# Conv taps and gated product kept in SBUF instead of PSUM, with other load buffers and another job order, in an attention and gated-projection kernel on one core

## The chip, the core and the metric

The kernel runs on one core of a Trainium2 chip. The metric is device time in microseconds (us), lower is better. The core's engines have queues of their own: TensorE (PE for the matmuls, PEld for the weight loads ahead of them), VectorE (DVE), ScalarE (ACT), GpSimd (POOL) and SyncE (SP, which issues the DMAs). PSUM is the memory that TensorE writes; SBUF is the large memory that all engines work in.

## What is computed

Rotary attention over 8 batches of 8 heads (sequence 576, head size 64), then a gated projection of the joined heads (width 512): a causal convolution of five taps per channel makes a gate, which multiplies a projected value, and a second projection gives the output.

```python
q_rot, k_rot = (rotate(q), rotate(k))
scores = scale * np.matmul(q_rot, k_rot.transpose(0, 1, 3, 2))
scores = scores - np.max(scores, axis=-1, keepdims=True)
attn = np.exp(scores)
attn = attn / (np.sum(attn, axis=-1, keepdims=True) + 1e-09)
x = np.matmul(attn, v)                      # heads joined: (8, 576, 512)
xp = np.concatenate([np.zeros((B, K - 1, D)), x], axis=1)
for k in range(K):                          # K = 5
    gate_pre += conv_w[k][None, None, :] * xp[:, k:k + S, :]
gate = 1.0 / (1.0 + np.exp(-gate_pre))
val = x @ w_val
return gate * val @ w_out
```

## The kernel before

**Tiling.** The 64 heads are 32 pairs `p`; a pair fills the 128 partitions. Four pairs make a batch `b`. Everything is transposed: channels on partitions, positions along the row. Matmul operands are split in a coarse part and a remainder (`hi`, `lo`), and three products of them are added, so most steps exist twice.

**One pair, in jobs.** `load` brings k and q, and `load_v` the values. `rope_mul` (two), `rope_add`, `qk_hi` and `qk_lo` make the rotated, split operands. `s_mm` computes the scores of two heads for 128 queries (12 matmuls, into two PSUM units), with `s_mix` for what is left over; `s_max` takes the row maximum on DVE and `s_exp` the exponential on ACT. `t_mm` turns the exponentials on TensorE, `t_copy` copies them to SBUF, `pv_mm` and `pv_left` multiply them with v, and `x_norm` writes the scaled result x. The reciprocal sums travel by `r_copy`, `r_write`, `r_read`. `x_hi` and `x_lo` split x. Five `tap` jobs and `gate` (a tanh) make the pair's gate.

**One batch.** `f_mm` of stage 0 multiplies with `w_val` (8 jobs of 6 matmuls into one unit). `y_mul` forms (gate + 1) times that unit, `y_hi` and `y_lo` split the product. Stage 1 multiplies with `w_out`; `o_out` scales and `o_dma` stores.

**PSUM units.** PSUM is cut in four units (`u`, two banks each). A score job takes two, and `t_mm`, `pv_mm` with the rest of its pair, `f_mm` and, before the change, the first `tap` take one. A unit is free again when the last reader of what it holds is done. The taps add into `ps_c` in such a unit until `gate` has read it; `y_mul` writes back into the unit of its `f_mm`, and `y_hi` and `y_lo` read it there.

**What sets the order.** `ORDER` is a table of about 3,100 job numbers. The jobs are issued in this order; within an engine they run in it. A letter behind a number picks the engine where several can do the job (V, A, G for DVE, ACT, GpSimd), and the digits behind a colon are the buffers or units that the job takes. `FILLS` puts idle transposes on TensorE at some steps. `Plan.run` has one more rule: a GpSimd job whose kind stands in `PAIRED` waits for the last DVE job of those kinds ahead of it in the table. Nothing makes a later DVE job wait for GpSimd.

**Lines.** L364 and L374 score matmuls, L384 turns, L480 and L490 products with v, L602 projections, L389 `s_max`, L398 `s_exp`, L467/L469 `t_copy` (ACT/DVE), L567/L569/L570 taps (DVE later ones, first one on DVE, on ACT), L582 gate, L615 `y_mul`, L626/L627 `y_hi` (DVE/ACT), L631 `y_lo`, L301 `rope_mul`, L305 `rope_add`, L326/L327 `qk_hi`, L333 and L336 `qk_lo` of q and k, L545/L546 `x_hi`, L552 `x_lo`.

Of the kernel before, what the change touches and what calls it, by code (L numbers as in the profile page):

```python
# [34 lines left out]
40 45:0 4 115 43:0 57:3 105A 147 116 23 44:0 48:2 5 58:1 119A 51:1 46:2 141G 59:1 49:3 47:2 54:3 142V 50 60:0 52:0 143G 63:2 55:1 53 148V 144A 66:1  # L35
64:2 56:3 145G 61:3 65 76:3 149V 67<61 216 77A:0 72:2 41 150V 62 74:3 106 73A 151V 78:0 152 146 75A:0 117 157:2 223 82V:0 79A 68:0 160:3 158:1 217G 69
154:0 161:2 159:0 166:1 155:3 70 162:2 218G 83:2 80 71 167:0 156 163:3 107 81A 169:0 168:1 219V 85 6 170:1 225G 90:1 87:0 377:100 220A 88:0 164:2 92
171:3 221V 165 184:0 224V 86A 292 84A 178:3 110A 229 118 175:2 185A:1 108 226V 89:0 179<108 172:0 176:3 227A 120G 93 180:0 177 109 222 91 194A:1 181
173:1 294V 174 192:2 186:3 293V 195 190:0 187A:1 228 94 295V 191A 299 239:3 95 182 193A 121G 236:0 196A 240:2 378A 305 183 241:0 237:3 197 131 230:1
198V 379 199:1 188:3 238:2 296V 200:1 233:2 380 189A 231:0 251:0 297G 234:1 232 248:3 381 235 488 262:1 111V 254:2 249:2 263A:0 112G 252:3 250:1 242:1  # L40
# [186 lines left out]
def attn_gated_ffn(ctx: ExitStack, tc: tile.TileContext, q2, k2, v2, tab, w_val, conv_w, w_out, out, collect=None):  # L227
# [326 lines left out]
    def tap(p, k, a, b, eng=V):  # L554
# [4 lines left out]
        if k == 0:  # L559
            st[f"c{a}"] = unit("ps_c")  # L560
# [385 lines left out]
```

## Time and profile before

| | |
|---|---|
| time, median of 3 runs (lowest to highest) | 675.24 us (674.88 to 679.53) |
| the profiled execution's own time | 675.39 us |
| span of its instructions | 673.6 us |
| PE / PEld busy | 648.9 / 534.9 us (96% / 79%) |
| DVE busy | 559.3 us (83%), 858 instructions |
| ACT busy | 474.8 us (70%), 1016 instructions |
| POOL busy | 299.9 us (45%), 239 instructions |
| mean granted TensorE clock | 0.982 of full speed |

A share is busy time over the span. Ends of matmuls are modelled, so 96% for PE doesn't say that it ran at its best rate; weight loads (PEld) run ahead of the matmuls that use them, and a wait shows at them first. A row of waits reads: engine, output tile and line that waited, `<-` what ended the wait, total us, times, longest.

### The profile page before, as it was taken

The page shows a single profiled execution, that of the slowest core. Times are in us where ns is not written, and L with a number is a line of the kernel's source. Part 1 is how long each engine was busy: PE and PEld are TensorE (multiplying, and loading weights), DVE is VectorE, ACT ScalarE, POOL GpSimd, SP SyncE. Part 2 cuts the span into 40 slices and gives each one's busy share as a digit, 9 for nine tenths or more (in the row PEclk, how much of TensorE's full clock was granted, in tenths as well). Part 3 has the DMA queues.
Part 4 walks back from the last instruction along what each step waited for, and adds up shares of the span by engine and source line. Part 5 has one row for each costly group of instructions (what it writes and reads, how often), then busy time and mean ns, then how long its engine had stood idle before and what let it go on. Part 6 is the DMA issues. An engine that isn't in the chain of part 4 may idle for free.

```text
span 673.6 us, 21213 instructions
## 1 busy us (share of the span) xinstructions
PE 648.9 (96%) x8937; PEld 534.9 (79%) x8937; DVE 559.3 (83%) x858; ACT 474.8 (70%) x1016; POOL 299.9 (45%) x239
## 2 busy tenths in 40 slices
PE   8999799999999999999999999999999999999997
PEld 6876567878787887967887889788778789689796
DVE  5899988899988988978987978888888888887762
ACT  4888978788778677567867677786668655767421
POOL 1424566566546455462525458325656225240000
PEclk9799979999999999999999999999999999999999
DMA  7355532533433244322432433443135423301202
GB/s 223 108 179 150 151 115 72 159 108 114 139 111 91 55 127 146 107 81 89 145 99 77 127 127 109 130 143 101 46 107 145 129 76 107 107 21 37 70 25 71
DMA packets 42721, 72.85 MB, mean 108 GB/s; under 512 B 15449, under 2 KB 18050, under 8 KB 42626
## 3 DMA queue, kind: packets, MB, share of 16 engines
q1 hardware_dynamic: 42082, 70.91, 34.0%
q8 instruction: 70, 1.15, 0.7%
q10 hardware_dynamic: 544, 0.59, 0.3%
q14 instruction: 25, 0.20, 0.1%
HBM read 61.89 MB, written 9.59 MB: 106 GB/s over the span
## 4 chain that ended last, share of the span: by engine, by line
PE 75%; DVE 9%; ACT 9%; DMA 4%; issue 2%; SPq 1%; DVEq 0%; ACTq 0%
PE ps_f L602 26%; PE ps_a L480 18%; PE ps_s L364 15%; PE ps_t L384 9%; PE ps_s L374 4%; ACT p L398 3%; DVE nm L389 3%; ACT pt L467 3%; PE ps_a L490 2%; DVE ps_c L567 1%; DMA rb<-rd 1%; DMA wst<-in_w_val 1%; DMA tab<-in_tab 1%; PE ps_s L384 1%; DMA qin<-in_q 1%
## 5 line engine op out<-in xcount | busy, mean ns | idle before, releaser
L389 DVE TENSOR_REDUCE nm<-ps_s 128x1 f32<-128x576 f32 x288 | 206.5, 751 | 49.6 <-PE ps_s L364 37.0
L398 ACT ACTIVATE p<-ps_s,nm 128x576 f32<-128x576 f32 x256 | 188.1, 740 | 59.2 <-DVE nm L389 58.2
L364 PE MATMUL ps_s<-k,q 64*128 64x288 f32 x1536 | 160.2, 312 | 8.3 <-ACT pt L467 2.9
L364 PEld LDWEIGHTS ps_s<-k,q 64*128 64x128 f32 x1536 | 131.8, 191 | 31.6 <-ACT p L398 12.4
L480 PE MATMUL ps_a<-pt,v 128*64 128x320 f32 (+1 forms) x1024 | 139.6, 418 | 0.3 <-ACT p L398 0.2
L467 ACT COPY pt<-ps_t 128x1024 f32<-128x1024 f32 (+1 forms) x125 | 114.8, 941 | 19.3 <-PE ps_t L384 18.2
L301 POOL TENSOR_TENSOR kin<-kin,tab 128x576 f32<-128x576 f32 x52 | 73.4, 1421 | 91.6 <-DMA kin<-in_k 35.9
L602 PE MATMUL ps_f<-y,wout_hi 64*128 64x288 f32 (+2 forms) x1024 | 110.3, 301 | 1.4 <-ACT o L637 0.5
L480 PEld LDWEIGHTS ps_a<-pt,v 128*64 128x64 f32 x1024 | 69.5, 139 | 50.2 <-issue 9.1
L567 DVE SCALAR_TENSOR_TENSOR ps_c<-x,cw,ps_c 128x576 f32<-128x576 f32 (+2 forms) x132 | 105.0, 801 | 4.4 <-ACT ps_c L570 1.3
L384 PE MATMUL ps_t<-ident,p 64*128 64x64 f32 x2172 | 94.7, 225 | 3.2 <-ACT p L398 1.5
L384 PEld LDWEIGHTS ps_t<-ident,p 64*128 64x128 f32 x2172 | 85.7, 139 | 13.2 <-ACT p L398 7.8
L301 POOL TENSOR_TENSOR qin<-qin,tab 128x640 f32<-128x640 f32 x40 | 62.1, 1562 | 64.2 <-DMA qin<-in_q 34.3
L602 PEld LDWEIGHTS ps_f<-y,wout_hi 64*128 64x128 f32 x1024 | 84.4, 185 | 6.2 <-issue 1.2
L602 PE MATMUL ps_f<-xh,wval_hi 64*128 64x288 f32 (+2 forms) x512 | 86.3, 308 | 1.7 <-ACT p L398 0.8
L602 PE MATMUL ps_f<-xl,wval_hi 64*128 64x288 f32 (+2 forms) x512 | 82.0, 292 | 0.1
L602 PE MATMUL ps_f<-xh,wval_lo 64*128 64x288 f32 (+2 forms) x512 | 82.0, 291 | 0.0
L602 PE MATMUL ps_f<-y,wout_lo 64*128 64x288 f32 (+2 forms) x512 | 79.7, 291 | 0.0
L602 PEld LDWEIGHTS ps_f<-xh,wval_hi 64*128 64x128 f32 x512 | 54.8, 185 | 4.9 <-ACT p L398 1.0
L602 PEld LDWEIGHTS ps_f<-xl,wval_hi 64*128 64x128 f32 x512 | 54.8, 185 | 0.3 <-DVE xl L552 0.3
L602 PEld LDWEIGHTS ps_f<-xh,wval_lo 64*128 64x128 f32 x512 | 54.7, 184 | 0.0
L552 POOL TENSOR_TENSOR xl<-x,xh 128x576 fp32r<-128x576 f32 x25 | 35.6, 1424 | 41.7 <-ACT xh L546 32.9
(107 smaller groups left out, 882.7 us busy)
## 6 DMA issues: line engine op xcount, KB each, us to landing
kin<-in_k SPq DMA_DIRECT2D x31, 576.0 KB
qin<-in_q SPq DMA_DIRECT2D x31, 512.0 KB
v<-in_v SPq DMA_DIRECT2D x32, 320.0 KB
out_t<-o SPq DMA_DIRECT2D x28, 288.0 KB
rb<-rd SPq DMA_DIRECT2D x31, 144.0 KB
rb<-rd SPq DMA_DIRECT2D x31, 128.0 KB
wst<-in_w_val SPq DMA_DIRECT2D x4, 512.0 KB
o<-in_w_out SPq DMA_DIRECT2D x4, 512.0 KB
```

The costliest lines, as they stand in the source:

```text
L301: return eng.tensor_tensor(out=t[:, i, a:b], in0=t[:, 0 if p < RAW else i, a:b], in1=table[:, i, a:b], op=ALU.mult)
L364: T.matmul(out=tiles[h][:, half, 0:288], lhsT=st["q"][HEAD[h], x, c * 128:c * 128 + 128], rhs=st["k"][HEAD[h], y, k0 + half * 288:k0 + hal ...
L374: inst = T.matmul(out=st["s8"][:, half], lhsT=st["q"][HEAD[h], x, 512:640], rhs=st["k"][HEAD[h], y, D + half * 288:D + half * 288 + 288], ...
L384: T.transpose(out=bank[0:src.shape[1], x, k * D:(k + 1) * D], in_=src[rows], identity=ident[rows, rows])
L389: return V.tensor_reduce(out=st[f"nm{i}"], in_=st[f"s{i}"], axis=AX.XY, op=ALU.max, negate=True)
L398: return A.activation(out=to.rearrange("p (b x) -> p b x", b=2), in_=st[f"s{i}"], func=AF.Exp, bias=st[f"nm{i}"], scale=1.0, accum_out=sum ...
L467: return A.copy(out=dst, in_=src)
L480: T.matmul(out=st[f"a{g}"][HEAD[h], 0:n], lhsT=st["v"][:, j, h, :], rhs=st[f"pt{g}"][:, h * 4 + j], start=(j == 0), stop=False)
L490: T.matmul(out=st[f"a{x}"][HEAD[h], 0:n], lhsT=st["v"][rows, 4, h, :], rhs=st["ptr"][rows, h, 0:n], start=False, stop=True)
L552: return eng.tensor_tensor(out=st["xl"][:, a:b], in0=xs[p % NX][:, 4 + a:4 + b], in1=st["xh"][:, a:b].bitcast(F32), op=ALU.subtract)
L567: return V.scalar_tensor_tensor(out=acc, in0=x_sb, scalar=w, in1=acc, op0=ALU.mult, op1=ALU.add)
L602: inst = T.matmul(out=acc[:, x, 0:hi - lo], lhsT=wt[w][HEAD[h], kc, dc * 128:(dc + 1) * 128], rhs=mv[HEAD[h], lo:hi], start=(turn == 0 and ...
```

## The change

The taps add in SBUF, in the tile `g` that later holds the gate, and so need no unit. The first tap writes `g`, four more read x and `g` and write `g`, and `gate` works on it in place. `y_mul` reads `g` and the projection's unit and writes the product into `g`; `y_hi` and `y_lo` read that, and `y_lo` may run on GpSimd too (`GV` for `V`). `tap`, `y_hi` and `y_lo` join the kinds in `PAIRED`. There are three x buffers for four, two v buffers for three, two k load buffers for one. `FILLS` gets four more transposes at step 73. The order table is another one: the same 3,100 jobs, with 21 of 36 `y_lo` on GpSimd (none before), 106 `rope_mul` and `rope_add` there (142 before; the others are on DVE), 21 `x_lo` (25), 23 `qk_lo` (21); 27 of the first taps on ACT (22).

```diff
-NX = 4
+NX = 3
+NV = 2
+NIN = {"k": 2, "q": 1}
...
-7 24 8 11 17 0:0 35 10 12V 153 13V 113 14:0 18V 9 25V 15 19V 26V 20:1 30V 104 36V 27:2 37V 31V 140 1 32:3 28 21 29 2 38:2 3 22 33 16 114A 34 42:1 39
+7 24 8 11 17 0:0 35 10 12V 113 13V 14:0 25V 18V 15 26V 1 30V 27:1 104 19V 140 31V 28 20:2 9 2 3 36V 32:3 16 37V 21 38:0 22 29 114A 45:2 23 115 33 39
...
-FILLS = {12: (20, 0)}
+FILLS = {11: (20, 0), 73: (4, 0)}
...
-    PAIRED = ("rope_mul", "rope_add", "qk_hi", "qk_lo", "x_hi", "x_lo", "weight_step")
+    PAIRED = ("rope_mul", "rope_add", "qk_hi", "qk_lo", "x_hi", "x_lo", "tap", "y_hi", "y_lo", "weight_step")
...
-    ins = {n: const.tile([128, 2, wide[n]], F32, name=f"{n}in") for n in "kq"}
+    ins = {n: [const.tile([128, 2, wide[n]], F32, name=f"{n}in{i}") for i in range(NIN[n])] for n in "kq"}
...
-    vs = [const.tile([128, 5, 2, D], F32, name=f"v{i}") for i in range(3)]
+    vs = [const.tile([128, 5, 2, D], F32, name=f"v{i}") for i in range(NV)]
...
-        if k == 0:
-            st[f"c{a}"] = unit("ps_c")
-        if b - a == S:
-            acc = st[f"c{a}"][:, :, 0:288]
-            x_sb = x_sb.rearrange("p (x n) -> p x n", x=2)
-        else:
-            acc = st[f"c{a}"][:, 0, 0:b - a]
-        if k:
-            return V.scalar_tensor_tensor(out=acc, in0=x_sb, scalar=w, in1=acc, op0=ALU.mult, op1=ALU.add)
-        if eng is V:
-            return V.tensor_scalar(out=acc, in0=x_sb, scalar1=w, scalar2=None, op0=ALU.mult)
-        return A.activation(out=acc, in_=x_sb, func=AF.Copy, scale=w)
...
         if "g" not in st:
             st["g"] = ring("pg", [128, S], F32, "g")
         g = st["g"][:, a:b]
...
+        if k:
+            return eng.scalar_tensor_tensor(out=g, in0=x_sb, scalar=w, in1=g, op0=ALU.mult, op1=ALU.add)
+        if eng is A:
+            return A.activation(out=g, in_=x_sb, func=AF.Copy, scale=w)
+        return eng.tensor_scalar(out=g, in0=x_sb, scalar1=w, scalar2=None, op0=ALU.mult)
...
+        g = state[p]["g"][:, a:b]
+        return A.activation(out=g, in_=g, func=AF.Tanh, scale=0.5)
...
     def y_mul(b, two, dc, lo, hi):
-        acc, g = halves(two, ffn[b, 0, two[0]], dc, hi - lo, state[b * PPB + dc]["g"][:, lo:hi])
-        return V.scalar_tensor_tensor(out=acc, in0=g, scalar=1.0, in1=acc, op0=ALU.add, op1=ALU.mult)
+        acc, y = halves(two, ffn[b, 0, two[0]], dc, hi - lo, state[b * PPB + dc]["g"][:, lo:hi])
+        return V.scalar_tensor_tensor(out=y, in0=y, scalar=1.0, in1=acc, op0=ALU.add, op1=ALU.mult)
...
-        return V.tensor_tensor(out=rest, in0=acc, in1=y.bitcast(F32), op=ALU.subtract)
+    def y_lo(b, dc, lo, hi, eng):
+        return eng.tensor_tensor(out=y_part(b, 1)[:, dc, lo:hi], in0=state[b * PPB + dc]["g"][:, lo:hi],
+                                 in1=ffn[b][0][:, dc, lo:hi].bitcast(F32), op=ALU.subtract)
...
-                add("V" if k else "AV", tap, p, k, a, b, r=xr + " cw", w=f"u/c{p}.{g}")
-            add("A", gate, p, a, b, r=f"u/c{p}.{g}", w=f"pg/{p}{part}")
+                add("V" if k else "AV", tap, p, k, a, b, r=xr + " cw", w=f"pg/{p}{part}")
+            add("A", gate, p, a, b, w=f"pg/{p}{part}")
...
-                        add("V", y_lo, b, two, dc, x, y, r=f"{mine} y0/{to}", w=f"y1/{to}")
+                        add("GV", y_lo, b, dc, x, y, r=f"{mine} y0/{to}", w=f"y1/{to}")
```

Where the order moves: DVE first, in the middle of the program, while the scores of pairs 16 and 17 are computed. Before, the taps of pair 15 (x_88) and pair 14 (x_87) stand like this; `nm<-ps_s` is a row maximum, `x2` a count:

```order
L389 TENSOR_REDUCE nm<-ps_s 128x1 x2
L567 SCALAR_TENSOR_TENSOR ps_c<-x_88,cw,ps_c 128x2x288
L326 TENSOR_SCALAR k_71<-kin 128x576
L567 SCALAR_TENSOR_TENSOR ps_c<-x_88,cw,ps_c 128x2x288 x3
L638 TENSOR_SCALAR o<-ps_f 128x576
L507 RECIPROCAL pm<-sums_89 128x9
L333 SCALAR_TENSOR_TENSOR q_73<-qin,q_73 128x640
L567 SCALAR_TENSOR_TENSOR ps_c<-x_87,cw,ps_c 128x2x288 x4
L389 TENSOR_REDUCE nm<-ps_s 128x1 x2
```

In the changed kernel the same place, with the taps of pair 13 (x_86) written to `g` (the lines have moved: L391 is the maximum, L565 the taps, L303 `rope_mul`, L471 `t_copy`):

```order
L391 TENSOR_REDUCE nm<-ps_s 128x1 x2
L565 SCALAR_TENSOR_TENSOR g<-x_86,cw,g 128x576
L303 TENSOR_TENSOR kin_69<-kin_69,tab 128x576
L391 TENSOR_REDUCE nm<-ps_s 128x1 x2
L471 COPY pt_5323<-ps_t 128x8x64
L471 COPY pr<-ps_t 64x2x64
L629 TENSOR_SCALAR o<-ps_f 128x576
L471 COPY pt_5344<-ps_t 128x2x8x64
L391 TENSOR_REDUCE nm<-ps_s 128x1 x2
L565 SCALAR_TENSOR_TENSOR g<-x_86,cw,g 128x576
```

Taps that stood in a row of four between two pairs of maxima now stand one by one, with a maximum pair, copies and rope work between.

GpSimd second, in the same part of the program, around the remainder of x of pair 12 (`xl<-x_85`). Before, its jobs are rope work (L301, L305), remainders of k (L336) and of x (L552), and the sums (L498):

```order
L336 TENSOR_TENSOR k_72<-kin,k_72 128x576
L301 TENSOR_TENSOR kin<-kin,tab 128x576
L552 TENSOR_TENSOR xl<-x_85,xh 128x576
L301 TENSOR_TENSOR qin<-qin,tab 128x640
L305 TENSOR_TENSOR qin<-qin 128x640
```

In the changed kernel (L303, L307 rope, L338 k, L554 x, L621 `y_lo`):

```order
L303 TENSOR_TENSOR kin_69<-kin_69,tab 128x576
L307 TENSOR_TENSOR kin_69<-kin_69 128x576
L303 TENSOR_TENSOR kin_70<-kin_70,tab 128x576
L621 TENSOR_TENSOR y_4827<-g,y_4803 128x576 x2
L554 TENSOR_TENSOR xl<-x_85,xh 128x576
```

Remainders of the gated product (`y<-g,y`) have come to GpSimd, and the k rope work alternates between two load buffers (kin_69, kin_70).

## Rows read from the trace of the kernel before

**Rows 1.** Engines by stage: us, busy us (count) of each, PEclk, DMA share, GB/s
```profile
0.00:130.00 130.00, 118.38 (x1302) 94.55 (x1304) 112.09 (x195) 103.59 (x220) 61.38 (x54) 0.91 0.48 143
...
130.00:640.00 510.00, 501.98 (x7241) 414.22 (x7239) 430.85 (x627) 365.21 (x782) 238.54 (x185) 1.00 0.33 103
...
640.00:674.00 34.00, 28.54 (x402) 26.17 (x398) 16.36 (x38) 5.97 (x14) 0.00 (x0) 0.99 0.14 47
```
**Rows 2.** Waits of the weight loads: who <- for whom: us, times, longest
```profile
PEld ps_s L364 <- ACT p L398: 12.4, 31, 0.6
...
PEld ps_t L384 <- ACT p L398: 7.9, 18, 0.8
...
PEld ps_s L364 <- ACT pt L467: 6.1, 10, 1.0
...
PEld ps_t L384 <- ACT pt L467: 3.6, 5, 1.2
...
PEld ps_s L364 <- ACT g L582: 2.2, 2, 1.7
...
PEld ps_f L602 <- ACT p L398: 1.5, 2, 1.0
...
PEld ps_s L364 <- ACT pm L398: 1.4, 3, 0.5
...
PEld ps_t L384 <- ACT pr L467: 1.4, 2, 0.9
```
**Rows 3.** Groups by shape: the taps and the tanh, the first product, its remainder
```profile
L567 DVE SCALAR_TENSOR_TENSOR ps_c<-x,cw,ps_c 128x576 f32<-128x576 f32 x124 | 101.0, 819 | 4.1 <-ACT ps_c L570 1.3
...
L582 ACT ACTIVATE g<-ps_c 128x576 f32<-128x576 f32 x31 | 20.3, 654 | 22.6 <-DVE ps_c L567 19.8 <-PE ps_f L602 2.6
...
L326 DVE TENSOR_SCALAR k<-kin 128x576 fp32r<-128x576 f32 x11 | 5.2, 470 | 0.0
...
L631 DVE TENSOR_TENSOR y<-ps_f,y 128x576 fp32r<-128x576 f32 x28 | 21.0, 750 | 2.5 <-ACT y L627 2.2
```
**Rows 4.** Timeline around 305 us: start, duration, engine, line, op, tiles, xcount
```profile
302.42 1.42 DVE L389 TENSOR_REDUCE nm<-ps_s 128x1 f32<-128x576 f32 x2 [0.54 <-PE ps_s L364]
...
302.81 1.95 PE L480 MATMUL ps_a<-pt,v 128*64 128x256 f32 x16
...
304.68 0.66 PE L374 MATMUL ps_s<-k,q 64*128 64x288 f32 x6
...
305.19 0.95 PE L364 MATMUL ps_s<-k,q 64*128 64x288 f32 x12
...
308.00 1.20 PE L384 MATMUL ps_t<-ident,p 64*128 64x64 f32 x32
...
309.01 1.19 PE L364 MATMUL ps_s<-k,q 64*128 64x288 f32 x12
```
**Rows 5.** Groups by shape: line, engine, op, tiles, xcount | busy us, mean ns | idle before
```profile
L389 DVE TENSOR_REDUCE nm<-ps_s 128x1 f32<-128x576 f32 x288 | 206.5, 751 | 49.6 <-PE ps_s L364 37.0 <-PE ps_s L374 8.3 <-PE ps_t L384 1.3
...
L398 ACT ACTIVATE p<-ps_s,nm 128x576 f32<-128x576 f32 x256 | 188.1, 740 | 59.2 <-DVE nm L389 58.2
...
L467 ACT COPY pt<-ps_t 128x1024 f32<-128x1024 f32 x103 | 102.2, 1016 | 17.8 <-PE ps_t L384 16.9
```
**Rows 6.** Lines 567, 333 and 301: duration ns min/median/max, first and last start us
```profile
L567 DVE SCALAR_TENSOR_TENSOR ps_c<-x,cw,ps_c x132: 478/823/824, 72.5 to 647.4; 128x576 f32<-128x576 f32 x124, 128x256 f32<-128x256 f32 x4, 128x320 f32<-128x320 f32 x4
...
L333 DVE SCALAR_TENSOR_TENSOR q<-qin,q x31: 762/817/2030, 24.8 to 600.1; 128x640 fp32r<-128x640 f32 x31
...
L301 POOL TENSOR_TENSOR kin<-kin,tab x52: 1401/1422/1444, 15.1 to 590.3; 128x576 f32<-128x576 f32 x52
```
**Rows 7.** Timeline near 438 us: DVE and POOL rows that overlap
```profile
438.36 1.56 POOL L305 TENSOR_TENSOR qin<-qin 128x640 f32<-128x640 f32 x1 [0.76 <-DVE kin L301]
...
438.81 1.73 DVE L305 TENSOR_TENSOR kin<-kin 128x576 f32<-128x576 f32 x1
```
**Rows 8.** Waits of GpSimd's k rope work for the k loads: us, times, longest
```profile
POOL kin L301 <- DMA kin<-in_k: 35.9, 7, 9.5
```

More of the change, by code (lines that the diff above doesn't have):

```diff
@@ L37 @@
[L37 to L40, printed above, removed]
@@ L313, in rope_mm @@
             for i, m in enumerate((ident, swap.rearrange("p h i x -> p (h i x)"))):
-                T.matmul(out=bank[:, (x - a) // h, 0:h], lhsT=m, rhs=ins[n][:, i, x:x + h], start=(i == 0), stop=(i == 1))
+                T.matmul(out=bank[:, (x - a) // h, 0:h], lhsT=m, rhs=ins[n][p % NIN[n]][:, i, x:x + h], start=(i == 0), stop=(i == 1))
     def rotated(p, n, a, b):
-        return state[p][f"b{n}{a}"] if p < RAW else ins[n][:, 0, a:b]
+        return state[p][f"b{n}{a}"] if p < RAW else ins[n][p % NIN[n]][:, 0, a:b]
     def like(p, t):
@@ L621, in y_part, with y_hi @@
         return parts[x]
-    def y_hi(b, two, dc, lo, hi, eng):
-        acc, y = halves(two, ffn[b, 0, two[0]], dc, hi - lo, y_part(b, 0)[:, dc, lo:hi])
+    def y_hi(b, dc, lo, hi, eng):
+        hi_, y = y_part(b, 0)[:, dc, lo:hi], state[b * PPB + dc]["g"][:, lo:hi]
         if eng is V:
-            return V.tensor_copy(out=y, in_=acc)
-        return A.copy(out=y, in_=acc)
-    def y_lo(b, two, dc, lo, hi):
-        acc, y, rest = halves(two, ffn[b, 0, two[0]], dc, hi - lo, ffn[b][0][:, dc, lo:hi], y_part(b, 1)[:, dc, lo:hi])
-        return V.tensor_tensor(out=rest, in0=acc, in1=y.bitcast(F32), op=ALU.subtract)
+            return V.tensor_copy(out=hi_, in_=y)
+        return A.copy(out=hi_, in_=y)
+    def y_lo(b, dc, lo, hi, eng):
+        return eng.tensor_tensor(out=y_part(b, 1)[:, dc, lo:hi], in0=state[b * PPB + dc]["g"][:, lo:hi],
+                                 in1=ffn[b][0][:, dc, lo:hi].bitcast(F32), op=ALU.subtract)
     def o_out(b, two, oc, lo, hi, eng):
@@ L718, in attn_gated_ffn @@
             V.memset(x_sb[:, 0:4], 0.0)
-        V.memset(ins["q"][D:128, :, 512:S], 0.0)
-        V.memset(ins["q"][0:D, :, S:W], 0.0)
+        for t in ins["q"]:
+            V.memset(t[D:128, :, 512:S], 0.0)
+            V.memset(t[0:D, :, S:W], 0.0)
     add = plan.add
@@ L871, in attn_gated_ffn @@
                         gp = PPB * b + dc
-                        mine = f"{acc}#{dc}" if last else acc
-                        add("V", y_mul, b, two, dc, x, y, r=f"{acc} pg/{gp}" + (half if gp == NP - 1 else ""), w=mine)
-                        add("AV", y_hi, b, two, dc, x, y, r=mine, w=f"y0/{to}")
-                        add("V", y_lo, b, two, dc, x, y, r=f"{mine} y0/{to}", w=f"y1/{to}")
+                        mine = f"pg/{gp}" + (half if gp == NP - 1 else "")
+                        add("V", y_mul, b, two, dc, x, y, r=acc, w=mine)
+                        add("AV", y_hi, b, dc, x, y, r=mine, w=f"y0/{to}")
+                        add("GV", y_lo, b, dc, x, y, r=f"{mine} y0/{to}", w=f"y1/{to}")
                     else:
```

270 lines of the change are left out of this document (134 added, 136 removed).

## The prediction, made before the changed kernel ran

> **What bounds the kernel now.** I read the engines by stage first [rows 1]. In the middle stage, from 130 to 640 us, PE is busy 502 of 510 us at a granted clock of 1.00. DVE is busy 431 us and ACT 365. So TensorE sets the pace there, but it is not at its best rate, since the ends of matmuls are modelled. In the first 130 us it is different: PE and its loads do less, the granted clock is 0.91, and DVE is busy 112 us. The last stretch is 34 us of projections without POOL.
>
> What TensorE loses in the middle stands in the waits of the weight loads [rows 2]. A score matmul reads k and q alone. When it waits for an exponential (`ACT p`, 12.4 us) or a copy of turned blocks (`ACT pt`, 6.1 us), what it waits for is a PSUM unit that this reader had to leave. The same holds for turning matmuls that wait for `pt` or `pr`, for projections that wait for `p`, and for scores that wait for the gate (`ACT g`, 2.2 us). Turning matmuls that wait for `p` (7.9 us) wait for data or for a unit. The eight rows, which are of the whole span, make 12.4 + 7.9 + 6.1 + 3.6 + 2.2 + 1.5 + 1.4 + 1.4 = 36.5 us. That is the amount that an easier supply of units can give back.
>
> **What the change removes.** Per pair, the taps hold one of the four units: a first tap, four more of 0.82 us and a tanh of 0.65 [rows 3], at least 0.75 + 3.28 + 0.65 = 4.7 us, which is about 150 us over 32 pairs, of 4 x 674 unit-us. The stage-0 units are free after `y_mul` and no longer wait for `y_hi` and `y_lo`; the latter alone took 0.75 us, 28 times [rows 3].
>
> Does it help that units are held for 150 us less? Only if units come round later than before, and that I read from the two order tables. I gave each TensorE job its time from start to start of neighbours in the timeline [rows 4]. A score job of 12 takes 309.01 to 309.92 us by what follows it, so 0.9. A block of 16 turns takes half of 308.00 to 309.01, so 0.5. Half a product with v takes 0.93 for the narrow kind, half of 302.81 to 304.68; I take 1.2 for the wide one, 0.7 for its rest and 0.4 for a projection job, from their neighbours in the same stretch. Then I summed, for each unit that held scores, the TensorE work between its last matmul and the next job that gets the unit. The mean is 2.56 us over 275 such reuses before, and 2.98 over 288 after. For units that held turned blocks it is 1.67 us (151) and 2.02 (163).
>
> What a score unit needs is a maximum of 0.75 us and an exponential of 0.74 [rows 5]. The second unit of a job needs one maximum more, so the mean is 1.9 us. A turned block needs its copy, 1.02 us on ACT, so 1.1. The work lacking below 1.9 and 1.1 us adds up to 36 + 10 = 46 us before, which is close to the 36.5 us of waits. After it adds up to 24 + 6 = 30 us, a third less. **Term 1:** a third of 36.5 us, 12 us back. Bounds: nothing, where the wait only moves on to the next reader, and all 36.5.
>
> **DVE's own work.** A tap read x from SBUF and its sum from PSUM: 819 ns [rows 3]. With both in SBUF, the nearest row is line 333, the same kind of instruction on 640 columns, with a median of 817 ns [rows 6]; for 576 columns that makes some 0.75 us. So 124 taps save 8.7 us. A first tap on DVE goes from 0.82 us towards the 0.47 us of the k split, an SBUF to SBUF scaling [rows 3]. Against this, 36 rope instructions move to DVE at about 0.8 us (+28 us), and 21 `y_lo` leave it (-16 us). With the smaller moves (copies, outputs, splits) my sum for DVE is 8 us less than before. DVE is not the bound in the middle stage (431 of 510 us), so I count a third: **term 2**, 3 us back, between 0 and 8.
>
> **What it adds.** Contention between DVE and POOL. The taps of before have a minimum, median and maximum of 478, 823 and 824 ns [rows 6] although, by my count over the trace, 84 of the 124 full ones overlap a POOL job of over 1 us: with one operand in PSUM they are never held up. Line 333, with two inputs in SBUF, has a median of 817 and a maximum of 2030 ns [rows 6]. At 438.8 us a `rope_add` on DVE took 1.73 us while a POOL job of 1.56 us had begun 0.45 us before it [rows 7]; its usual time is 0.75. It ended just after that POOL job and its own 0.75 us. The changed taps, `y_hi` and `y_lo` become such instructions. `PAIRED` makes POOL start behind them; but the next one on DVE starts when its turn comes, and must sit out the rest of a POOL job of 1.42 us [rows 6].
>
> I counted how much POOL work is not covered, between one such DVE job and the next, by DVE work that can't collide (two maxima in a row cover 1.42 us [rows 4]). It is 22 us before and 54 after. In the trace of before, the DVE instructions above the usual time of their kind exceed it by some 8 us (some 18 instructions, of which the two named are examples), so about 0.4 of what is uncovered. 54 x 0.4 is 22 us, 14 more than now. A third of that on TensorE's path, as above, gives **term 3**, 4 to 5 us lost; bounds 0 and all 32 us more.
>
> The Trainium skill, in "SBUF — State Buffer", section "Who interferes with whom", says that a DVE instruction with two SBUF inputs and a GpSimd instruction that reads SBUF exclude each other, and that the second to issue waits for the whole of the first. The trace agrees in the row of 1.73 us. By that rule alone every uncovered microsecond is a wait, which is the rival below that ends slower.
>
> **Costed at nothing.** Two k load buffers: POOL's rope work waited 35.9 us for k loads [rows 8], but by the order the split k stands a mean of 17 us of TensorE work ahead of its scores; what hides the wait is POOL's idle time (239 of 510 us busy in the middle stage [rows 1]). If that cover went, the first score job of a pair would be late by one POOL job, 1.42 us. Fewer v and x buffers: v is still loaded a good 8 us of TensorE work ahead of its use, and the taps of a pair are done before x of the third next pair is written. Four fill transposes: under 1 us, in a stretch where TensorE waits for DVE. `gate` and the first taps on ACT change by some 0.03 us each. The first 130 us: DVE has the same work ahead of pair 4's end in both orders (102 and 101 us in my sum), so I give no gain there; nor in the last 34 us.
>
> **Sum.** 675.4 us of the profiled execution, which is 0.2 above the median, less 12, less 3, plus 4 to 5, makes 664 to 665; on the median 664.
>
> **The rivals.** *The units were nearly everything.* Two thirds of the 36.5 us go, since the waits at exponentials come from the whole rotation and not only from the unit the taps hold: 675 - 24 - 3 + 4 = 652, and 650 with some of the smaller waits. For it: taps are now spread out in the order, and no longer sit four in a row in front of a maximum. Against it: PE is idle only 8 us in the middle stage [rows 1].
>
> *The lock decides.* The 32 us more of uncovered POOL time all become DVE waits, and a late tap makes the maximum behind it late, then the exponential, then the unit. The place is each tap that follows a POOL job in the middle stage. All of it on the path gives 675 - 15 + 32 = 692, three quarters 684. It is slower by over 1% from 22 us on the path, two thirds of the 32. For it: POOL's work has more neighbours to collide with than before. Against it: DVE idles 79 us in the middle stage, and a DVE that is held up in an idle stretch costs nothing.
>
> *It does nothing.* Units come free earlier, but what TensorE waits for is the rate of ACT and DVE in the score stretches, two exponentials, 1.5 us, for 0.9 us of score matmuls. The waits stay, and terms 2 and 3 cancel: 673 to 677.
>
> **How the numbers follow.** A measurement of this kernel tells about 1% from no change, 6.8 us. My sum: chance 0.40, 655 to 668. The units: 0.18, about 650. The lock: 0.20, taken between three quarters and all of it, about 686. Nothing: 0.22, about 674. So faster by over 1% has 0.40 + 0.18 = 0.58, within 1% 0.22, slower 0.20. The likeliest case is 664, its own range 655 to 668. A range for 8 in 10 leaves out half of the first rival and half of the lock's case: 648 to 686.
>
> **What would show it.** In the profile after: the tile `ps_c` is gone; taps have a median near 0.75 us, and their maximum tells of the lock (over 1.5 us where it bites); the eight kinds of waits of the weight loads fall from 36 to about 24 us; `y<-g,y` runs on POOL in some 1.4 us; the first 130 us last as long as before, and the middle stage is the shorter one. I am wrong if the waits at units stay and the time falls elsewhere, if the gain lies in the first 130 us, or if taps are stretched in number and the maxima behind them late.

## The result and the profile after

The changed kernel takes 658.5 us (median of 4 runs, 658.1 to 659.5). The kernel before, run beside it, takes 675.4 (4 runs, 674.9 to 679.5). The ratio is 0.974, with a 95% interval of 0.970 to 0.978: it is faster by 2.6%, about 17 us. The profiled execution took 658.7 us with a span of 657.0, where before it was 675.4 with a span of 673.6.

The engines by stage come first. The three stretches answer to [rows 1]; the last two are cut at 625 us, since the end comes 17 us earlier. The columns are those of [rows 1].

```profile
0.00:130.00 130.00, 118.59 (x1324) 94.91 (x1324) 117.34 (x198) 104.79 (x227) 48.16 (x44) 0.92 0.48 147
130.00:625.00 495.00, 491.49 (x7225) 411.98 (x7225) 425.36 (x647) 362.70 (x774) 222.11 (x173) 1.00 0.34 105
625.00:657.00 32.00, 27.41 (x399) 26.43 (x396) 15.63 (x35) 6.37 (x14) 3.18 (x4) 0.98 0.14 48
```

TensorE gets through nearly as many matmuls as before (7225, before 7241) in a middle stage that is cut 15 us shorter, and is still the busy one. DVE is as busy as before over the whole span (558.3 us, before 559.3), and so is ACT (473.9, before 474.8), so the gain isn't a matter of less work for either. POOL has 26 us less.

To see where the time went I took as marks the last part of a pair's product with v (eight matmuls), for pair 4 and for pair 28. The rows are of that line alone: duration in ns, minimum, median and maximum, then the first and the last start in us. First the kernel before, then the changed one.

```profile
L490 PE MATMUL ps_a<-pr,v x8: 376/428/481, 111.2 to 111.6; 64*64 64x256 f32 x4, 64*64 64x320 f32 x4
...
L490 PE MATMUL ps_a<-pr,v x8: 376/428/480, 587.4 to 587.7; 64*64 64x256 f32 x4, 64*64 64x320 f32 x4
```

```profile
L492 PE MATMUL ps_a<-pr,v x8: 376/428/481, 108.1 to 108.4; 64*64 64x256 f32 x4, 64*64 64x320 f32 x4
...
L492 PE MATMUL ps_a<-pr,v x8: 376/428/480, 571.5 to 571.8; 64*64 64x256 f32 x4, 64*64 64x320 f32 x4
```

Up to pair 4 the changed kernel is 3.1 us ahead (111.2 to 108.1). From pair 4 to pair 28 it takes 463.4 us where before it took 476.2, so 12.8 us come there. The rest is 85.5 us of the span against 86.2: 0.7 us. The sum is 16.6.

The waits of the weight loads answer to [rows 2] (us, times, longest us):

```profile
PEld ps_s L366 <- ACT p L400: 10.0, 25, 0.6
PEld ps_t L386 <- ACT p L400: 6.7, 16, 0.9
...
PEld ps_t L386 <- ACT pt L469: 4.3, 4, 1.8
PEld ps_s L366 <- ACT pr L469: 3.7, 3, 2.8
PEld ps_s L366 <- ACT pt L469: 3.4, 7, 0.8
...
PEld ps_s L366 <- ACT g L573: 0.5, 1, 0.5
...
PEld ps_f L593 <- ACT p L400: 0.5, 1, 0.5
```

The eight kinds of [rows 2] made 36.5 us. The same kinds are now 25.6: scores behind `p` fell from 12.4 to 10.0, turns behind `p` from 7.9 to 6.7, scores behind `pt` from 6.1 to 3.4, scores behind the tanh from 2.2 to 0.5, projections behind `p` from 1.5 to 0.5, and the two rows of 1.4 are nothing and 0.2. Turns behind `pt` rose a little, from 3.6 to 4.3, and scores behind `pr` rose from 0.3 to 3.7. A sum over chosen kinds can mislead, so here is the whole: all waits of the weight loads that ended with ACT, DVE or POOL make 63.1 us before and 45.6 after.

A second count gives every instruction of the trace to its job. Between pair 4 and pair 28 both kernels run 834 TensorE jobs. What these last, from start to start, beyond the shorter ones of their kind (the 20th percentile over all the runs) is 50 us before and 37 after. Of this, 27 and 17 us end just as (within 0.3 us) the last reader leaves a unit that the next matmul needs. That is 9.5 of the 12.7 us that the middle gained by this count.

The taps and the remainder of the product answer to [rows 3] and [rows 6]:

```profile
L565 DVE SCALAR_TENSOR_TENSOR g<-x,cw,g x132: 478/814/1468, 53.1 to 639.5; 128x576 f32<-128x576 f32 x124, 128x256 f32<-128x256 f32 x4, 128x320 f32<-128x320 f32 x4
...
L621 POOL TENSOR_TENSOR y<-g,y x21: 732/1419/1432, 128.2 to 641.4; 128x576 fp32r<-128x576 f32 x17, 128x256 fp32r<-128x256 f32 x2, 128x320 fp32r<-128x320 f32 x2
L621 DVE TENSOR_TENSOR y<-g,y x15: 427/750/982, 274.1 to 644.4; 128x576 fp32r<-128x576 f32 x11, 128x256 fp32r<-128x256 f32 x2, 128x320 fp32r<-128x320 f32 x2
```

The median tap takes 814 ns, before 823. The longest takes 1468, where before none took over 824. 21 of the 36 remainders run on POOL, in 1.42 us.

### The profile page after: what moved, and what is told of

It reads as the page before. It is cut to its first block, busy times and chain, and to the rows that moved or that the text cites. A ratio compares the mean times of both kernels' runs of the same rounds, so it can differ in the third digit from the quotient of the medians.

```text
span 657.0 us, 21249 instructions
## 1 busy us (share of the span) xinstructions
PE 637.5 (97%) x8941; PEld 533.3 (81%) x8941; DVE 558.3 (85%) x877; ACT 473.9 (72%) x1014; POOL 273.4 (42%) x221
## 4 chain that ended last, share of the span: by engine, by line
PE 84%; ACT 6%; DVE 5%; DMA 2%; issue 1%; POOL 1%; SPq 1%; ACTq 0%; DVEq 0%; POOLq 0%
PE ps_f L593 30%; PE ps_a L482 18%; PE ps_s L366 16%; PE ps_t L386 11%; PE ps_s L376 4%; PE ps_a L492 3%; ACT p L400 2%; DVE nm L391 2%; ACT pt L469 2%; DMA v<-in_v 1%; PE ps_r L316 1%; PE ps_s L386 1%; DMA rb<-rd 1%; PE ps_f L407 1%; DVE g L565 1%
## 5 line engine op out<-in xcount | busy, mean ns | idle before, releaser
L391 DVE TENSOR_REDUCE nm<-ps_s 128x1 f32<-128x576 f32 x288 | 206.0, 751 | 39.9 <-PE ps_s L366 31.9
L366 PE MATMUL ps_s<-k,q 64*128 64x288 f32 x1536 | 154.2, 311 | 6.6 <-ACT pr L469 3.2
L366 PEld LDWEIGHTS ps_s<-k,q 64*128 64x128 f32 x1536 | 128.9, 192 | 23.6 <-ACT p L400 10.0
L469 ACT COPY pt<-ps_t 128x1024 f32<-128x1024 f32 (+1 forms) x131 | 122.3, 946 | 26.0 <-PE ps_t L386 24.0
L482 PE MATMUL ps_a<-pt,v 128*64 128x320 f32 (+1 forms) x1024 | 136.8, 412 | 0.4 <-ACT p L400 0.3
L565 DVE SCALAR_TENSOR_TENSOR g<-x,cw,g 128x576 f32<-128x576 f32 (+1 forms) x132 | 107.7, 826 | 1.7 <-ACT g L567 0.7
L386 PEld LDWEIGHTS ps_t<-ident,p 64*128 64x128 f32 x2172 | 88.5, 140 | 14.8 <-ACT p L400 5.8
L386 PE MATMUL ps_t<-ident,p 64*128 64x64 f32 x2172 | 97.0, 226 | 2.6 <-ACT pt L469 1.6
L593 PEld LDWEIGHTS ps_f<-y,wout_hi 64*128 64x128 f32 x1024 | 84.8, 186 | 3.8 <-issue 1.5
L593 PE MATMUL ps_f<-xh,wval_hi 64*128 64x288 f32 (+2 forms) x512 | 84.5, 306 | 0.1
L303 POOL TENSOR_TENSOR qin<-qin,tab 128x640 f32<-128x640 f32 x39 | 60.5, 1561 | 40.2 <-DVE g L565 16.6
L303 POOL TENSOR_TENSOR kin<-kin,tab 128x576 f32<-128x576 f32 x31 | 43.9, 1421 | 53.7 <-DVE g L565 22.0
L554 POOL TENSOR_TENSOR xl<-x,xh 128x576 fp32r<-128x576 f32 x21 | 29.9, 1425 | 54.5 <-DVE xh L547 39.3
```

The costliest lines, as they stand in the source:

```text
L303: return eng.tensor_tensor(out=t[:, i, a:b], in0=t[:, 0 if p < RAW else i, a:b], in1=table[:, i, a:b], op=ALU.mult)
L366: T.matmul(out=tiles[h][:, half, 0:288], lhsT=st["q"][HEAD[h], x, c * 128:c * 128 + 128], rhs=st["k"][HEAD[h], y, k0 + half * 288:k0 + hal ...
L386: T.transpose(out=bank[0:src.shape[1], x, k * D:(k + 1) * D], in_=src[rows], identity=ident[rows, rows])
L391: return V.tensor_reduce(out=st[f"nm{i}"], in_=st[f"s{i}"], axis=AX.XY, op=ALU.max, negate=True)
L469: return A.copy(out=dst, in_=src)
L482: T.matmul(out=st[f"a{g}"][HEAD[h], 0:n], lhsT=st["v"][:, j, h, :], rhs=st[f"pt{g}"][:, h * 4 + j], start=(j == 0), stop=False)
```

## The experiments

Theory *units*: TensorE loses time because it waits for PSUM units, the change gives units back earlier, and so it gains. Its main rival is *rate*: the pace is that of ACT and DVE, and units follow. Beside these stand the two DVE terms (a tap's length, the lock with POOL) and the start. They ran in three groups (the four with copies behind the exponentials; the late copies, the old order and the constant; the other four), each on one chip with runs of the kernel before, whose medians were 674.5, 673.9 and 675.9 us. So kernels of different groups are best compared by their ratios.

| kernel | median us | ratio to before, 95% interval | pair 4 ends | pair 4 to 28 | rest | DVE busy us |
|---|---|---|---|---|---|---|
| before | 675.4 | 1 | 112.0 | 476.1 | 85.5 | 559.3 |
| changed | 658.5 | 0.974 (0.970 to 0.978) | 108.8 | 463.4 | 84.8 | 558.3 |
| before, units held by one copy | 680.5 | 1.008 (1.005 to 1.011) | 112.7 | 478.7 | 86.2 | 557.9 |
| before, same copies, units free | 679.6 | 1.009 (1.005 to 1.012) | 111.8 | 479.2 | 85.6 | 559.7 |
| before, units held by one job | 742.5 | 1.100 (1.097 to 1.103) | 128.3 | 522.7 | 89.3 | 558.4 |
| changed, units held by one copy | 666.3 | 0.986 (0.980 to 0.991) | 113.5 | 467.7 | 84.9 | 558.6 |
| changed, same copies, units free | 664.3 | 0.984 (0.980 to 0.988) | 109.1 | 467.7 | 85.0 | 559.2 |
| changed, units held by one job | 731.5 | 1.084 (1.081 to 1.087) | 126.8 | 513.3 | 88.8 | 557.1 |
| SBUF taps in the old order | 722.7 | 1.071 (1.069 to 1.074) | 115.6 | 516.9 | 87.1 | 610.2 |
| changed, constant tap scalar | 658.3 | 0.975 (0.972 to 0.977) | 108.9 | 462.9 | 84.7 | 550.2 |
| changed, POOL not held behind taps | 667.0 | 0.987 (0.983 to 0.990) | 111.1 | 472.7 | 84.5 | 570.5 |
| changed, remainders all on DVE | 661.5 | 0.978 (0.975 to 0.982) | 108.3 | 466.3 | 84.6 | 568.6 |
| before, one ACT job moved | 674.2 | 0.998 (0.995 to 1.000) | 109.1 | 477.3 | 86.2 | 559.4 |
| changed, no second fill | 660.7 | 0.977 (0.973 to 0.980) | 108.8 | 463.8 | 84.8 | 560.6 |

The four columns behind the ratio are of each kernel's profiled execution: the end of pair 4's last product matmul, the time from there to pair 28's, what is left of the span, and DVE's busy time.

### Units held a little longer, and the same work without holding

The edit puts a tiny ACT copy behind every exponential, in the kernel before and in the changed one. It reads a column of the score unit, which then can't be reused until the copy is done; in its twin it reads an SBUF column.

```diff
-        return A.activation(out=to..., in_=st[f"s{i}"], func=AF.Exp, ...)
+        inst = A.activation(out=to..., in_=st[f"s{i}"], func=AF.Exp, ...)
+        A.activation(out=warm, in_=st[f"s{i}"][:, 0, 0:1], func=AF.Copy)
+        return inst
```

In the twin the added line reads `in_=warm`.

> The kernel before with one tiny ACT copy behind every exponential of scores (288 of them), which reads one column of the score unit and so keeps that PSUM unit from reuse for the length of one copy more, about 0.2 us. Theory units (TensorE is held up because it waits for a PSUM unit to be read out): the trace of before has 56 weight loads that wait for an exponential; each ends about 0.2 us later, so this run is some 8 to 12 us slower than its twin whose copy reads SBUF (before_ctrl). Rival rate (what counts is how fast ACT and DVE get through their work, and the units follow): the two are within 2 us of each other.

> The kernel before with the same 288 tiny ACT copies, but reading an SBUF column, so that ACT has the same work and no PSUM unit is held longer. Theory units: some 8 to 12 us faster than before_hold; against the kernel before it pays only ACT's 58 us of extra work, which ACT (474 of 674 us busy) has room for in most places: 0 to 10 us. Rival rate: within 2 us of before_hold.

> The changed kernel with the copy that holds the score unit. Its trace has 48 weight loads that wait for an exponential. Theory units: 5 to 10 us slower than after_ctrl, and less than the same difference in the kernel before, because the change has left the units more room. Rival rate: within 2 us of after_ctrl.

> The changed kernel with the copy that reads SBUF. Theory units: 5 to 10 us faster than after_hold, 0 to 10 us slower than the changed kernel without copies. Rival rate: within 2 us of after_hold, and both well slower than the changed kernel.

Measured: 680.5 against 679.6 before, and 666.3 against 664.3 after, differences that lie within the intervals. By the numbers put down, *rate* had it. But the test was weaker than I had thought. Each copy ended only 0.06 us behind the accumulator read that belongs to the exponential (17.6 us over 288 copies), and not the 0.2 us that I had assumed, since the copy starts while that read is still running:

```profile
305.66 0.19 ACT L398 ACTIVATION_READ_ACCUMULATOR p<-ps_s,nm 128x1 f32 x1
305.75 0.16 ACT L400 ACTIVATE warm<-ps_s 128x1 f32<-128x1 f32 x1
```

Between pair 4 and pair 28 this little hold cost nothing that shows (478.7 and 479.2; 467.7 and 467.7). The twins aren't quite the same work: their copies end 0.09 us behind the read, and ACT is busy 23 us longer than without copies, where the copies that hold add 16. By the price of ACT's time below, that hides about 1 us. The 2 us of the changed kernel's pair come ahead of pair 4, where the granted clock differs. These rows are the first 130 us with the copies that hold, then with those that don't:

```profile
0.00:130.00 130.00, 117.76 (x1270) 94.37 (x1272) 112.83 (x191) 102.54 (x273) 45.64 (x43) 0.88 0.46 142
```

```profile
0.00:130.00 130.00, 116.98 (x1320) 93.19 (x1322) 117.58 (x197) 108.69 (x283) 47.69 (x44) 0.92 0.48 147
```

What the twins do show is a price of ACT's time: 23 us more on ACT, with no unit read by the copies, cost 3 to 4 us between pairs 4 and 28 in both kernels.

### Units held by one ACT job

The same copies, each moved behind the next ACT job (or, where the unit's next tile comes first in the order, put just ahead of that).

```diff
+        inst = A.activation(out=to..., in_=st[f"s{i}"], func=AF.Exp, ...)
+        late.append((st[f"at{i}"], st[f"s{i}"][:, 0, 0:1]))
+        return inst
...
+            held = [x for x in self.late] if on == "A" else []
             inst = fn(*args, *([engine[on]] if len(engines) > 1 else []))
+            for x in held:
+                self.read_out(x[0])
```

`read_out` emits the copy; `unit` calls it for a slot before it hands the slot out again.

> The kernel before with the same 288 tiny ACT copies as before_hold, but each placed behind the next ACT job that follows its exponential (where the unit's next tile does not come first), so 214 score units are given back one ACT job later, some 0.9 us each or 190 unit-us in all, for the same ACT work as before_ctrl. Theory units: time given back to the units is what the change gains by; at the change's own price (waits 12 us less for the 155 unit-us of the taps and about as much of the product) this costs some 10 to 20 us over before_ctrl. Rival rate: within 2 us of before_ctrl.

> The changed kernel with the same late copies: 239 score units given back one ACT job later. Theory units: 10 to 20 us over after_ctrl, so that most of what the change gained is gone again. Rival rate: within 2 us of after_ctrl.

Measured: 62.8 us over the twin in the kernel before, 67.2 in the changed one (by the ratios, as the twins ran in another group, 61 and 67). *Rate* falls: ACT is as busy as in the twins, to 3 us, and 196 and 221 us of unit time (ends of the copies less ends of the accumulator reads, summed) cost a tenth of the whole time. The waits stand where the theory says. By the count over jobs, 73 and 66 us between the marks end with a unit's reader, in the twins 29 and 20: that is all of the difference there. First the twin of before, whose waits for `p` and for the copy `warm` make 24.3 us in four rows, then the kernel with the late copies, where three rows make 79:

```profile
PEld ps_s L364 <- ACT p L398: 7.4, 20, 0.6
...
PEld ps_s L364 <- ACT warm L400: 6.3, 14, 0.5
PEld ps_t L384 <- ACT p L398: 5.4, 15, 0.8
PEld ps_t L384 <- ACT warm L400: 5.2, 11, 0.5
```

```profile
PEld ps_s L378 <- ACT warm L272: 36.1, 64, 1.2
PEld ps_t L398 <- ACT warm L272: 34.2, 54, 1.8
PEld ps_f L619 <- ACT warm L272: 8.8, 10, 1.8
```

And the changed kernel with the late copies:

```profile
PEld ps_s L380 <- ACT warm L274: 36.1, 66, 1.2
PEld ps_t L400 <- ACT warm L274: 26.8, 45, 1.4
```

The size was four times what I expected. Part of it, 16.5 and 17.7 us, comes ahead of pair 4, where the clock is at the lower of its two levels, 1.2 GHz, for 48 us in each, in place of 17 and 20. Between pair 4 and pair 28 it is 43.5 us before and 45.6 after. Some 139 and 165 us of the held time lie there, which makes 0.31 and 0.28 us per unit-us. That is well above the change's own price, 12 us for some 150 unit-us of taps; a likely reason, not tested, is that a unit that waits for another job also waits for what that job waits for. Two things follow. Holding units longer is dear, though a hold of 0.06 us cost nothing that shows. And the changed kernel is as sensitive as the one before: the change left little of what it freed as a reserve. Counted from a tile's first matmul or tap to its last reader's end, units were occupied for 1714 of 1904 unit-us between pair 4 and pair 28 before, and for 1622 of 1854 after. Of the 145 unit-us of taps that went, 42 are idle time now, 53 went to scores and 14 to turned blocks; the rest went with the shorter stretch. That a longer hold costs doesn't show by itself that an earlier release gains; for that there are the counts of the changed kernel above.

### The SBUF taps in the old order

The changed kernel's taps, tanh and product in SBUF, with the job order, the buffers and the one fill of the kernel before.

```diff
-NX = 3
-NV = 2
-NIN = {"k": 2, "q": 1}
+NX = 4
+NV = 3
+NIN = {"k": 1, "q": 1}
-FILLS = {11: (20, 0), 73: (4, 0)}
+FILLS = {12: (20, 0)}
```

The order table is that of before, with the slots of `pg` set at the first tap and every `y_lo` marked V.

> Taps and gated product in SBUF as in the changed kernel, but in the job order, with the load buffers (four x, three value, one key) and the early transposes of the kernel before; the low parts of the product all on DVE, as before. So the units are relieved and nothing else is moved. Theory relief alone: most of the 12 us of unit waits go whatever the order, 661 to 667 us. Theory relief through the order: units that come free where the old order has no job for them help little, 670 to 676 us. Rival lock: DVE's taps with both operands in SBUF are stretched by POOL and it is slower than before, 677 to 685 us.

Measured: 722.7 us, 7% slower than before. All three expectations were too low; the lock is the one with the right sign, and its 48 us are five times the most that I gave it. The busy times of the page:

```profile
PE 661.5 (92%) x8937; PEld 542.3 (75%) x8937; DVE 610.2 (85%) x858; ACT 476.8 (66%) x1016; POOL 313.5 (44%) x239
```

DVE has the jobs of before and is busy 51 us longer. The taps, which in PSUM had a maximum of 824 [rows 6]:

```profile
L567 DVE SCALAR_TENSOR_TENSOR g<-x,cw,g x132: 474/819/2227, 70.3 to 694.3; 128x576 f32<-128x576 f32 x124, 128x256 f32<-128x256 f32 x4, 128x320 f32<-128x320 f32 x4
```

The median is the old one, but 38 of the full taps take over 1 us, and what they take above 0.82 is 39 us. Two rows of POOL show what happens to three taps in a row (start, duration, engine):

```profile
227.90 5.32 DVE L567 SCALAR_TENSOR_TENSOR g<-x,cw,g 128x576 f32<-128x576 f32 x3
...
228.79 1.56 POOL L305 TENSOR_TENSOR qin<-qin,tab 128x640 f32<-128x640 f32 x1 [1.55 <-DVE g L567]
231.04 1.57 POOL L305 TENSOR_TENSOR qin<-qin,tab 128x640 f32<-128x640 f32 x1 [0.69 <-DVE g L567]
```

Three taps of 0.82 make 2.5 us, and the two POOL jobs 3.1 more: 5.6, where 5.3 are measured. A POOL job starts as the tap that it was held behind ends, and the next tap has to sit it out. That one of the two waits for the whole of the other is the rule of the Trainium skill that the prediction quoted ("SBUF — State Buffer", "Who interferes with whom"), and these rows agree with it. Its other half, that the second to issue is the one to wait, can't be read here: taken one by one, the rows of the second and third tap start at 228.75 and 231.00, 0.04 us ahead of the POOL rows, and yet it is the taps that wait. What can be read is the end. All 63 taps over 1 us, of this kernel, the changed one and the next, end 0.61 to 0.62 us after the POOL job that they sat through. The maxima, which read PSUM, were not touched:

```profile
L393 DVE TENSOR_REDUCE nm<-ps_s x288: 690/748/759, 14.1 to 678.7; 128x1 f32<-128x576 f32 x144
```

So the relief alone is a large loss. In the old order 84 of the taps ran beside a POOL job and it cost nothing; with both operands in SBUF 57 still do, and it costs more than the units give. The new order has 20 such taps, 8 of them over 1 us. By the count over jobs, 45 us of TensorE's time between the marks end with a unit's reader, where the kernel before has 27: the lock reaches TensorE as waits for units that are read late. What I had taken for the part that merely rearranges is what makes the change pay. Whether the gain of the order, with its buffers and its fill, over this kernel (64 us) is all the lock, or partly a better use of the units, was not taken apart.

### POOL not held behind taps

```diff
-    PAIRED = (..., "x_hi", "x_lo", "tap", "y_hi", "y_lo", "weight_step")
+    PAIRED = (..., "x_hi", "x_lo", "weight_step")
```

> The changed kernel, but POOL no longer waits for the tap, y_hi or y_lo that stands ahead of it in the job order (the list of paired jobs is that of the kernel before); the order itself and the engines are as they are. In the changed kernel 22 POOL jobs wait for a tap, 66 us in all. Theory lock: these jobs now start under the taps, whose operands both lie in SBUF, and stretch them; the run of the old order had taps of 1.13 us on average in place of 0.85; DVE's busy time rises by 10 to 40 us and the time to 664 to 690 us. Rival: the waits only hold POOL up and cost nothing to lose, 655 to 660 us with taps as long as they are.

Measured: 667.0 us, a ratio to before of 0.987 where the changed kernel has 0.974: the waits of POOL are worth 8.5 us, with some 3.6 either way. It is the lock, near the lower end of what was put down. The page and the taps:

```profile
PE 642.1 (96%) x8941; PEld 534.2 (80%) x8941; DVE 570.5 (85%) x877; ACT 474.2 (71%) x1014; POOL 291.2 (44%) x221
```

```profile
L565 DVE SCALAR_TENSOR_TENSOR g<-x,cw,g x132: 476/810/2214, 55.3 to 650.8; 128x576 f32<-128x576 f32 x124, 128x256 f32<-128x256 f32 x4, 128x320 f32<-128x320 f32 x4
```

DVE is busy 12 us longer and POOL 18: here the POOL jobs are stretched too. 17 taps take over 1 us, in place of 8. Between the marks 25 us end with a unit's reader, in place of 17, which is most of the 9.3 us lost there. Holding POOL back behind DVE instructions looks like a cost in the waits of the changed kernel (these four largest rows are 22 POOL jobs that wait 66 us for taps), and it is a gain:

```profile
POOL kin L303 <- DVE g L565: 22.0, 7, 6.4
POOL qin L303 <- DVE g L565: 16.6, 7, 7.0
POOL kin L307 <- DVE g L565: 15.0, 5, 5.1
...
POOL k L338 <- DVE g L565: 12.3, 3, 5.6
```

### A constant in place of the tap's column

```diff
-            return eng.scalar_tensor_tensor(out=g, in0=x_sb, scalar=w, in1=g, op0=ALU.mult, op1=ALU.add)
+            return eng.scalar_tensor_tensor(out=g, in0=x_sb, scalar=0.25, in1=g, op0=ALU.mult, op1=ALU.add)
```

> The changed kernel, but taps 1 to 4 multiply by the constant 0.25 in place of the weight column (so the convolution's weights are left out for those four taps; all else as it is). The prediction took a tap with both operands in SBUF to be about 0.75 us, and it is 0.81. If the column operand is what makes the difference, the taps' median is 0.74 to 0.76 here, DVE has some 8 us less to do, and by the prediction's rule (a third of DVE's own saving shows) the time falls by 2 to 3 us below the changed kernel. Rival: the length is that of the two-step operation whatever its scalar, the median stays at 0.81 and the time does not move.

```profile
L565 DVE SCALAR_TENSOR_TENSOR g<-x,g x132: 415/750/1333, 54.4 to 639.1; 128x576 f32<-128x576 f32 x124, 128x256 f32<-128x256 f32 x4, 128x320 f32<-128x320 f32 x4
```

```profile
PE 636.6 (97%) x8941; PEld 532.3 (81%) x8941; DVE 550.2 (84%) x877; ACT 474.0 (72%) x1014; POOL 274.9 (42%) x221
```

The first half came out as put down: the median is 750 ns in place of 814, so the column costs 64 ns per tap, and DVE has 8.1 us less to do. The second half did not show. The time is 658.3, as with the column, and 462.9 us between the marks, where it was 463.4. Eight microseconds of DVE work taken from the taps are worth nothing that can be measured here; but the two ratios leave some 3 us either way, so the 2 to 3 us of the rule aren't excluded.

### The remainders on DVE

The 21 `y_lo` that the changed order has on POOL go to DVE (`436G` becomes `436V`, and so on).

> The changed kernel with all 36 low parts of the product on DVE; 21 were on POOL. DVE gets some 14 us more to do (0.77 each), POOL 25 to 28 us less. By the prediction's rule, that a third of DVE's own work shows in the time, it is 4 to 5 us slower than the changed kernel: 662 to 664 us. Rival: DVE has room where these stand, as the constant-scalar run suggests (7 us less tap time gained nothing there): 657 to 660 us.

```profile
PE 638.7 (97%) x8941; PEld 532.5 (81%) x8941; DVE 568.6 (86%) x898; ACT 474.6 (72%) x1014; POOL 249.2 (38%) x200
```

The median is 661.5, 2.9 us above the changed kernel, but the two ratios (0.978 and 0.974) have intervals that overlap. The profiled executions agree on 2.9 between pair 4 and pair 28. DVE got 10.3 us more and not 14, so its other instructions took some 4 us less, with 24 us less of POOL beside them. That would be 0.3 us per microsecond added, as by the prediction's rule, but it isn't shown.

### The start

> The kernel before with one ACT job moved: the first step of decoding weight block 1, which waits for its DMA until 11.9 us, goes behind the rounding of the last query part, which TensorE's second score tile waits for. In the changed kernel the first maximum starts 1.4 us earlier, and some 4 us of its gain come in the first 40 us. Theory start: the first maximum comes 1 to 1.5 us earlier here too and stays so to the end, 672 to 673 us, ratio 0.997 to 0.999. Rival: the lead is lost within the first pairs, where other waits end last, and the time is that of before.

```diff
-16 114A 34 42:1 39
-40 45:0
+16 34 42:1 39 114A
+40 45:0
```

> The changed kernel without the four identity transposes at step 73 of the order. Theory clock: they keep TensorE busy in a gap of the first 20 us, so without them one more 3.4 us stretch, or a longer one, runs at the lower of the two clock levels, and it is 1 to 3.5 us slower: 660 to 662 us. Rival: they do nothing, 657.5 to 659.5 us.

```diff
-FILLS = {11: (20, 0), 73: (4, 0)}
+FILLS = {11: (20, 0)}
```

Both are inconclusive as to time: 674.2 us, with an interval that reaches 1.000, and 660.7, with one that overlaps the changed kernel's. The timelines tell more. First the start of the kernel before (the weight transfer's issue, the first decoding step, the first maximum), then with the one job moved, then the changed kernel:

```profile
6.36 0.81 SPq L696 DMA_DIRECT2D wst<-in_w_val  x2
...
11.89 0.66 ACT L654 ACTIVATE wst<-wst 128x512 f32<-128x512 f32 x1 [1.22 <-DMA wst<-in_w_val]
...
13.61 0.75 DVE L389 TENSOR_REDUCE nm<-ps_s 128x1 f32<-128x576 f32 x1
```

```profile
12.12 0.66 ACT L654 ACTIVATE wst<-wst 128x512 f32<-128x512 f32 x1 [0.34 <-DMA wst<-in_w_val]
...
12.81 0.43 DVE L660 TENSOR_SCALAR wst<-wst 128x512 int32<-128x512 int32 x1 [0.49 <-ACT wst L654]
...
13.15 0.75 DVE L389 TENSOR_REDUCE nm<-ps_s 128x1 f32<-128x576 f32 x1
```

```profile
4.92 1.75 SPq L687 DMA_DIRECT2D wst<-in_w_val  x2
...
9.70 0.66 ACT L645 ACTIVATE wst<-wst 128x512 f32<-128x512 f32 x1
...
12.25 0.75 DVE L391 TENSOR_REDUCE nm<-ps_s 128x1 f32<-128x576 f32 x1
```

Moving ACT's job brought 0.5 us and not 1.4, because DVE's second decoding step stands ahead of the first maximum and waits for the same transfer. In the kernel before, the start of that maximum hangs on when the transfer lands (in its twin with free copies, which issues it at the same 6.36 us, the decoding step started at 10.56 us without a wait and the maximum at 12.32). The changed order issues the weights ahead of the v load, 1.4 us earlier, and the maximum started between 12.20 and 12.31 us in all kernels with that order. That much is the order's doing. How much of it lives on to pair 4 stays open: pair 4 ended at 109.1 to 112.7 us in kernels with the old order and at 108.3 to 113.5 with the new one (late copies and SBUF taps left out), and the time at the lower clock level ahead of 130 us, 14 to 24 us and 20 to 31, moves as much. Without the second fill the total at the lower level is the same 20 us, only elsewhere.

Not tried: each order needs its own count of x, v and k buffers, since loads and uses are ordered for it, so the buffers could not be had without the order. Nor was there a run of the new order with the taps left in PSUM, so what relief and order are worth one by one is not known.

## Why the prediction was right, and where not

The forecast was 664 us and faster, with 655 to 668 as the likeliest case's own range and 648 to 686 for 8 in 10. It is 658.5, with the sign as forecast, inside both ranges, and with the gain mainly where it was looked for: in the middle, in waits for units. The sum of 11 us was 6 us short.

**Term 1, 12 us from the units: held.** The waits of [rows 2] fell by 11 us, to near the 24 of the forecast, and all waits of the weight loads behind ACT, DVE and POOL by 17.5. By the count over jobs, 9.5 us of the gain between pairs 4 and 28 are time that ended with a unit's reader. That units held longer cost time is shown by the late copies. What is not shown is that the freed tap units alone bring it: in the old order they were free as well and it was slower, so the term is one of relief and order together. The rule by which I got the size, a third of the waits from a third of the lacking work, is one that the runs don't test; a price per unit-us, which I didn't use, is nothing to rely on, as it went from 0 to 0.3 with the length of the hold.

**Term 2, 3 us from DVE's own work: wrong in the saving, open in its price.** The step that failed is the nearest row, line 333 [rows 6], from which I took 0.75 us for a tap. That instruction has a constant as its scalar, and the tap has a column. With a constant the tap is 750 ns, with its column 814, and 812 where no POOL job runs beside it. So moving both operands to SBUF saved some 10 ns each, the stretched ones more than ate that up (the 124 full taps make 105.0 us, before 101.5), and DVE's busy time fell by 1 us and not by 8. The other part, a third of DVE's saving on the path, stays open: it came out as 0 in the run with the constant and as about 0.3 in the run that added work, and both lie within some 3 us of noise, so the two don't contradict each other or the third.

**Term 3, 4 to 5 us lost to the lock: right in kind, too high here, and far too small as a danger.** By the count that gave 8 us of stretch before, the changed kernel has some 14, where I expected 22, and the old order with SBUF taps 62. The 0.4 of uncovered POOL time that I took from before is too much, as `PAIRED` now sends POOL off behind taps and products, into the maxima. Without that, DVE is busy 12 us longer and the time is 8.5 us more. My reading of [rows 7] was a little off as well: the `rope_add` ended 0.62 us after the POOL job, and not its own 0.75. What the prediction did not see is the other end: its rival *the lock decides* stopped at 692, and the same taps in the old order give 723. I weighed the order as a change of the unit rotation, when it also keeps POOL from under the taps (20 taps beside a POOL job, where the old order has 57), and without that the change doesn't pay.

**Costed at nothing.** The stretch up to pair 4 is 3 us shorter, where I gave none; the first maximum is earlier by the weights' earlier issue, but a lasting gain isn't shown. The tail gave 0.7. POOL's 35.9 us of waits for k loads [rows 8] are gone, its waits for q loads fell from 34.3 to 6.5, and no new wait for a load is among the 30 longest; the buffers stay untested by themselves.

**The sum by measured terms.** 12.8 in the middle, 3.1 at the start and 0.7 at the end make the 16.6. Against the forecast, the middle is some 2 us better than the 10 to 11 that 12 + 3 less 4 to 5 make, and the rest of what was missing lies outside of it.

## What to carry to other kernels

Here buffers given back earlier paid only together with a new order of the work. What the moved operands do to other engines can cost more than the buffers bring, so test the relief in the old order before you credit it. Where DVE instructions with two SBUF inputs run beside GpSimd work, read their maximum and not their median, and place GpSimd's jobs under DVE instructions that read PSUM. When you price an instruction by a neighbour's row, look at every operand, the scalar too.

## What the runs showed of the hardware

- A `scalar_tensor_tensor` of 128 x 576 took 814 ns with a column as its scalar and 750 with a constant, all else alike; whether its second tensor lay in PSUM (823) or in SBUF (814) made little difference.
- Such a tap with both tensors in SBUF, beside a POOL job of 1.56 us, took up to 2.2 us, and every stretched one ended 0.61 to 0.62 us after the POOL job. The same tap with one tensor in PSUM never took over 0.82, though 84 of them ran beside POOL jobs. POOL's jobs are held up as well, 2.07 us for one of 1.56 in the run without the waits.
- A tiny ACT copy behind an exponential ended only 0.06 us after the accumulator read where it read PSUM (0.09 where it read SBUF), and 288 of them made ACT busy 16 us longer (23), 0.055 us each (0.08), though each is shown as 0.17 us long (0.195).
